# A chunked attention recurrence and its MLP: four small matrix products laid into quarters of TensorE, denser loads of a, r and v, and a new order of all engines

## The chip, the cores and the metric

The kernel runs on one core of a Trainium2 chip. The metric is the device time of one execution in microseconds (us), as a median of several runs. The engines are named as in the profile: PE (TensorE, matrix products; PEld is its loading of weights), DVE (VectorE), ACT (ScalarE), POOL (GpSimd) and SP (SyncE, which here only issues transfers).

## What is computed

For each of 4 x 8 heads a 40 x 40 state goes through 768 steps; the outputs of all heads, 320 numbers a token, then go through an MLP:

```python
for t in range(S):
    y[:, :, t] = np.einsum('bhd,bhde->bhe', rt, state)
    Sa = np.einsum('bhde,bhe->bhd', state, at)
    state_decay = state * wt[:, :, None, :] - np.einsum('bhd,bhe->bhde', Sa, bt)
    state = state_decay + np.einsum('bhd,bhe->bhde', vt, kt)
...
x = np.ascontiguousarray(attn_out.transpose(0, 2, 1, 3)).reshape(B * S, H * D)
a = x @ w1
b = x @ w2
h = a * b @ w3
return (h @ w_out).astype(np.float32)
```

S = 768, D = 40, B = 4, H = 8; w1 and w2 are 320 x 1024, w3 1024 x 1024, w_out 1024 x 320. The MLP's weights arrive as 64-bit floats.

## The kernel before, in words

The 768 steps are cut into 12 chunks c of 64 tokens. The 32 heads are 16 pairs: a batch entry is a group g (four of them) of four pairs p, and a pair's two heads lie in partitions 0 to 39 and 64 to 103 (`ab` = 0, 1 in the code). Of each chunk these steps are made, the first ones for each group:

- `load` (L369) fetches w, b and k (`fm`) and a (`lh`, which stands twice, each time with one head's rows filled and the other's zero).
- `scale` (L374): a running product of w on DVE (L386), its logarithm and inverse on ACT (L390, L393), and with these a (L397) and b, k (L408, "x scaling") are multiplied; L397 and L408 are on DVE or POOL by a letter per chunk in `ON`.
- `causal` (L420): one full-array product per pair of scaled b, k with scaled a (L431). ACT copies parts of it into `JP` and the rest back into `lh`, where POOL cuts off the upper triangle (L449).
- `solve` (L455), once for the chunk's 16 pairs together: the inverses of the triangular 64 x 64 matrices, by some 40 DVE instructions that wait for one another, from the transpose L463 (which reads all four groups' `JP`) to the transposes L538 and L541 (which write `TDX`). `join` (L545) completes the inverses with two PE products (L564, L571) and ACT copies into `TT`.
- `pairs` (L591): r times v, the "small products" (L608), copied by ACT and cut by POOL (L616). `tokens` (L620) transposes b and k on PE (L631).
- `rec` (L636), the recurrence itself: state (L647, the state `SB` times r and a's identity part), two ACT copies into `xu`; f2 (L654), a copy into `hs`; inverse (L661, `TT` times `hs`); two masks on DVE back into `xu` (L665); f5 (L672); the new state and y on DVE (L689, L706), a transpose on PE (L695), two copies into `SB`.
- `gather` (L710) collects y by transfers into `xr`, and `mlp` (L727), some two chunks later, has 16 products with W1, W2 (L758, eight matmuls each), DVE products of the two (L772), `gh` and the rest `gl` (L775), and eight products with W3 w_out (L784).

At the start `weights` (L310) turns the 64-bit weights into pairs of floats: 33 pieces of 128 x 512 go through `convert` (L268), four or five passes on DVE, two on ACT and one on POOL (L298). The product of w3 and w_out is made once (L351). The MLP of the first chunk waits for all of them.

PE lays the shapes out as follows: L431, L647, L631, L695 and the MLP use the full array; L654 and L672 two column halves; L608 and L661 two of the four 64 x 64 quarters beside each other; L564 and L571 two of the 32 x 32 parts.

The order of all instructions is not written out by hand. Every operation is given an engine, a cost and a due time (`Order.op`, L70); `place` (L89) puts them one by one, always the one that can start first and among these the one due first, with the buffers of `SLOTS` (L30) and the costs as its clock. What comes out is fixed as a queue for each engine, in that order. `T` and `P` (L35, L36) hold the due times.

Of the kernel before, what the change touches and what calls it, by code (L numbers as in the profile page):

```python
# [24 lines left out]
TOK = B * C  # L25
W65 = C + 1
WMAX, GMIN = 1.5, 2.0 ** -40
CW = 512
LAT = dict(pe=0.33, act=0.09, dve=0.09, pool=0.1, sp=3.0, nil=0.0)
SLOTS = dict(fm=8, lh=6, gi=2, gt=1, ab=1, TDX=1, rv=3, xu=3, bk=3, hs=2, st=2, y=1, xr=1, JP=2, TT=2, bank=6,  # L30
# [4 lines left out]
T0, T = 29.92, 49.86  # L35
P = dict(w0=14.16, ws=3.0, ld=73.16, sc=53.09, ca=46.04, so=7.66, sp=36.36, jo=7.42, pa=12.28, tk=5.03, rg=13.65,  # L36
         ga=35.51, ml=86.47, mt=47.69)

ON = dict(cv="p", ws="d", lh="ppddpppppddp", xs="pppdpppppppd", gl="pppdpddddddd")


class Slot:


    def __init__(self, order, pool):
        self.order, self.pool, self.at, self.left, self.since, self.until = order, pool, None, 0, 0.0, 0.0
        if order.direct:
            self.at = order.turn[pool] = (order.turn.get(pool, -1) + 1) % SLOTS[pool]

    @property  # L50
    def t(self):
        return self.order.tiles[self.pool][self.at]


class Order:
# [11 lines left out]
    def slot(self, pool):  # L67
        return Slot(self, pool)

    def op(self, eng, cost, due, fn, r=(), w=(), two=False, kind=None, hold=()):  # L70
# [11 lines left out]
        slots = {k[0] if isinstance(k, tuple) and isinstance(k[0], Slot) else k for k in (*r, *w, *hold)}  # L82
        slots = [s for s in slots if isinstance(s, Slot)]
        for s in slots:
            s.left += 1
        self.ops.append(dict(n=n, eng=eng, cost=cost, due=due, fn=fn, deps=deps - {None, n}, slots=slots, two=two,
                             kind=kind))

    def place(self):  # L89
# [28 lines left out]
        placed = []  # L118
        while len(placed) < len(ops):
            best = None  # L120
            for e in LAT:
                starts = [(t, o) for o in ready[e] if (t := begin(o)) is not None]
                if starts:
                    first = min(t for t, _ in starts)
                    o = min((o for t, o in starts if t <= first + 1e-9), key=lambda o: (o["due"], o["n"]))
                    if best is None or first < best[0]:
                        best = first, o
            if best is None:
                raise ValueError(f"stuck after {len(placed)} of {len(ops)}: " + str([(e, o["due"], o["fn"].__qualname__, [(s.pool, s.at) for s in o["slots"]]) for e in LAT for o in sorted(ready[e], key=lambda o: o["due"])[:4]]) + str({p: len(f) for p, f in free.items()}))
            t, o = best  # L130
            e = o["eng"]
            ready[e].remove(o)
            cost = o["cost"]
            if e == "pe":
                cost += 0.1 * (o["kind"] != last)
                last = o["kind"]
            for s in o["slots"]:
                if s.at is None:
                    at = min(free[s.pool])
                    free[s.pool].remove(at)  # L140
                    s.since, s.at = at
# [3 lines left out]
            done = clock[e] + LAT[e]  # L145
            o["start"], o["end"] = t, clock[e]
            placed.append(o)
            for s in o["slots"]:
                s.until, s.left = max(s.until, done), s.left - 1
                if not s.left:  # L150
                    free[s.pool].append((s.until, s.at))
            for u in o["users"]:
                u["wait"] -= 1
                u["ready"] = max(u["ready"], clock[e] if u["eng"] == e != "sp" else done)
                if not u["wait"]:
                    ready[u["eng"]].append(u)
        self.placed = sorted(placed, key=lambda o: (o["start"], o["n"]))
# [4 lines left out]
def attention_moe(ctx: ExitStack, tc: tile.TileContext, fmx, fma, rv, vt, sq, svr, w12, w3t, wo, out):  # L162
# [44 lines left out]
    SB = cp.tile([104, NPC, 104], F32, name="SB")  # L207
# [9 lines left out]
    for name, shape in dict(fm=[104, 772], lh=[128, 2, NP, C], gi=[104, NP, C], gt=[104, NP, C],   # L217
                            TDX=[128, 1024], rv=[104, NP, 2 * C + D], xu=[128, 2, NP, C + D], bk=[128, NP, 104],
# [48 lines left out]

    def convert(src, dst, due, w=()):  # L268

        n = src.shape[1]  # L270
        raw, e, sg, mf = slot("raw"), slot("e"), slot("sg"), slot("mf")

# [21 lines left out]
        def f7():  # L294
            dve.tensor_tensor(out=sg.t[:, 0:n], in0=sg.t[:, 0:n], in1=e.t[:, 0:n].bitcast(BF16), op=ALU.mult)
# [4 lines left out]
        op("sp", 0.6, due - 8, f1, w=[raw])  # L300
# [4 lines left out]
        op("dve", 0.64, due, f6, r=[raw], w=[mf], two=True)  # L305
        op("dve", 0.38, due, f7, r=[e], w=[sg], two=True)
        both(ON["cv"], 1.25, 0.62, due, f8, r=[sg, "conv"], w=[mf] if dst is None else [mf, *w])
        return mf

    def weights():  # L310

        due, step = P["w0"], P["ws"]
        for k in range(3):
# [13 lines left out]
            for f in range(2048 // CW):  # L327
                cs = slice(CW * f, CW * f + CW)
                mf = convert(w12[k * 128:k * 128 + 128, cs], None, due)
                n = (0, 1, 4)[k]  # L330
                rows = slice(64, 128) if k == 2 else slice(0, 128)
                over = ["conv"] if k == 0 else ["conv", "reg2"]

                def f1(mf=mf, n=n, cs=cs):
                    copy(WT[n][:, cs], mf.t)

                def f2(e, mf=mf, n=n, rows=rows, k=k, cs=cs):
                    e.tensor_tensor(out=WT[2 + k][rows, cs], in0=mf.t[rows], in1=WT[n][rows, cs], op=ALU.subtract)
# [22 lines left out]
    fm_, lh_, jp_, tt_, xu_, rv_, bk_, y_, xr_, tdx_ = ({} for _ in range(10))  # L361
# [7 lines left out]
    def load(c, g, due):  # L369
        fm, lh = fm_[c, g], lh_[c, g] = slot("fm"), slot("lh")  # L370
        op("sp", 0.6, due, lambda: sp.dma_start(out=fm.t, in_=fmx[c, g]), w=[(fm, "g"), (fm, "x")])
        op("sp", 0.4, due, lambda: sp.dma_start(out=lh.t[0:104], in_=fma[c, g]), w=[(lh, 0), (lh, 1)])

    def scale(c, g, due):  # L374

        fm, lh, gi, gt = fm_[c, g], lh_[c, g], slot("gi"), slot("gt")
# [18 lines left out]
        def f5(e):  # L395
            a = lh.t[0:104]
            e.tensor_tensor(out=a, in0=a, in1=gam(c, g)[:, :, 0:C].unsqueeze(1).to_broadcast([104, 2, NP, C]), op=ALU.mult)  # L397
# [17 lines left out]
        both(ON["lh"][c], 1.2, 0.62, due + 1, f5, r=[G], w=[(lh, 0), (lh, 1)])  # L415
        op("dve", 0.42, due + 2, f6, r=[G, gi], w=[gt], two=True)
        op("dve", 0.45, due + 2, f7, r=[gt], w=[gi], two=True)
        both(ON["xs"][c], 1.35, 0.62, due + 3, f8, r=[gi], w=[(fm, "x")])

    def causal(c, g, due):  # L420

        fm, lh, jp, pt = fm_[c, g], lh_[c, g], jp_[c], slot("bank")
        ns = slice(g * NP, g * NP + NP)

        def bank():
            return pt.t.rearrange("p (n x t) -> p n x t", n=NP, x=2)

        def f1():
            X = x12(c, g)
            for p in range(NP):  # L430
                pe.matmul(out=bank()[:, p], lhsT=X[:, p].rearrange("q x t -> q (x t)"), rhs=lh.t[0:104, :, p],  # L431
                          start=True, stop=True)

        op("pe", 0.92, due, f1, r=[(fm, "x"), (lh, 0), (lh, 1)], w=[pt], kind="128", hold=[jp])
        for ab in range(2):
            q = 64 * ab
            op("act", 0.39, due + 1, lambda q=q, ab=ab: copy(
                jp.t[q:q + 32, ns], bank()[q:q + 32, :, ab].rearrange("q p (x t) -> q p x t", x=2)),
               r=[pt], w=[(jp, g, 2 * ab)])
            op("act", 0.29, due + 1, lambda q=q, ab=ab: copy(  # L440
                jp.t[q + 32:q + 64, ns, 0], bank()[q + 32:q + 64, :, ab, 32:64]), r=[pt], w=[(jp, g, 2 * ab + 1)])
        for ab in range(2):
            q = slice(64 - 64 * ab, 128 - 64 * ab)

            def f2(q=q, ab=ab):
                copy(lh.t[q, ab], bank()[q, :, ab], -1.0)
# [5 lines left out]
            op("act", 0.4, due + 4, f2, r=[pt], w=[(lh, ab)])  # L452
            op("pool", 0.5, due + 6, f3, w=[(lh, ab)], two=True)

    def solve(c, due, span):  # L455
# [28 lines left out]
        def dots(out_, x, y, shape, slow=1.0):  # L484
# [30 lines left out]
        for z in range(2):  # L515
# [3 lines left out]
                 lambda r0=r0: A()[:, r0:r0 + 8, r0 + 8:r0 + 16].unsqueeze(2), (8, 4, 8), 1.8)  # L519
# [439 lines left out]
```

## Time and profile before

| | |
|---|---|
| median of 3 runs | 761.85 us (759.58, 761.85, 767.97) |
| the profiled execution | 762.65 us, of which the span of the profile is 760.9 |
| busy: PE, weight loads, DVE, ACT, POOL | 650.0, 584.3, 597.3, 474.0, 249.7 us |
| chain of work that ended last | PE 61%, DVE 25%, transfers 8%, ACT 3% |
| transferred | 70.29 MB in 57,937 packets, mean 92 GB/s |
| per issue: fm, rv, lh, a piece of weights | 313.6, 273.0, 208.0, 512.0 KB |

A row of groups reads: line, engine, operation, output <- inputs, shapes, count | busy us, mean ns of one | idle time just before them and what ended it. A row of the timeline: start, duration, then the same. PE's instructions overlap, so how long one holds the engine is read from start to start. A float product is two passes, so two MATMUL records: L661 has 16 for its eight products.

### The profile page before, as it was taken

The numbers are of one execution on the slowest core, as the hardware profiler recorded it, in microseconds if no ns is written. First come the engines' busy times: TensorE is split into PE (matmuls) and PEld (weight loads), VectorE is DVE, ScalarE is ACT, GpSimd is POOL, SyncE is SP. The second block draws the span as 40 slices with busy tenths as digits, with TensorE's granted clock in tenths as the row PEclk, the third lists the DMA queues.
The fourth block names the chain that finished last, engine by engine and source line by source line (L and its number), as shares of the span: only waits on it lengthen the run. The fifth ranks groups of instructions, "written<-read, shape, count | busy, mean of one in ns | idle before, by whom it ended". The sixth has DMA issues, their size and how long they took to land.

```text
span 760.9 us, 20122 instructions
## 1 busy us (share of the span) xinstructions
PE 650.0 (85%) x7954; PEld 584.3 (77%) x7954; DVE 597.3 (78%) x1173; ACT 474.0 (62%) x1127; POOL 249.7 (33%) x330
## 2 busy tenths in 40 slices
PE   2323777848689999999999998999999999999996
PEld 1312655636579889898899987998989989998996
DVE  5679989999989985895978967968898799783321
ACT  3474575456767568676696775775957768654331
POOL 3356333544424154362433622513223222100000
PEclk9955669968779999999999999999999999999999
DMA  8922364623440151532424324224243242210010
GB/s 205 262 70 67 118 182 152 178 85 108 110 114 15 32 148 38 134 86 71 109 68 119 81 55 108 83 69 122 58 109 90 68 111 80 48 52 19 21 28 20
DMA packets 57937, 70.29 MB, mean 92 GB/s; under 512 B 30960, under 2 KB 38640, under 8 KB 57840
## 3 DMA queue, kind: packets, MB, share of 16 engines
q1 hardware_dynamic: 57840, 68.97, 33.6%
q8 instruction: 64, 1.05, 0.6%
q14 instruction: 33, 0.27, 0.1%
HBM read 60.29 MB, written 3.93 MB: 84 GB/s over the span
## 4 chain that ended last, share of the span: by engine, by line
PE 61%; DVE 25%; DMA 8%; ACT 3%; issue 2%; SPq 0%; DVEq 0%
PE bank L758 21%; PE bank L784 10%; PE bank L431 5%; PE bank L654 4%; PE bank L647 4%; PE bank L661 4%; PE bank L672 4%; DVE tmp L489 3%; DVE mf L291 3%; PE bank L608 3%; DMA fm<-in_fmx_dram 2%; DMA rv<-in_rv_dram 2%; DVE xu L665 2%; DMA lh<-in_fma_dram 2%; PE bank L695 2%
## 5 line engine op out<-in xcount | busy, mean ns | idle before, releaser
L758 PE MATMUL bank<-xs,W 128*128 128x256 f32 x1536 | 214.5, 289 | 1.0 <-ACT lh L173 1.0
L758 PEld LDWEIGHTS bank<-xs,W 128*128 128x128 f32 x1536 | 191.0, 190 | 7.2 <-issue 2.4
L173 ACT ACTIVATE xu<-bank 64x256 f32<-64x256 f32 (+2 forms) x184 | 80.3, 441 | 47.2 <-PE bank L647 21.1
L616 POOL TENSOR_SCALAR_AFFINE_SELECT xu<-xu 64x256 f32<-64x256 f32 x96 | 45.1, 470 | 143.2 <-ACT xu L173 122.3
L173 ACT ACTIVATE JP<-bank 32x256 f32<-32x256 f32 (+1 forms) x216 | 75.7, 351 | 22.4 <-PE bank L431 17.6
L408 POOL TENSOR_TENSOR fm<-fm,gi 104x512 f32<-104x512 f32 x40 | 57.7, 1441 | 69.4 <-DVE gi L404 60.7
L431 PE MATMUL bank<-lh,fm 104*128 104x128 f32 x384 | 59.6, 305 | 22.1 <-POOL fm L408 16.0
L665 DVE TENSOR_TENSOR xu<-bank,mask_h 64x416 f32<-64x416 f32 x96 | 56.2, 585 | 25.9 <-PE bank L661 24.1
L431 PEld LDWEIGHTS bank<-lh,fm 104*128 104x128 f32 x384 | 53.3, 214 | 24.7 <-POOL fm L408 16.8
L449 POOL TENSOR_SCALAR_AFFINE_SELECT lh<-lh 64x256 f32<-64x256 f32 x96 | 42.8, 445 | 85.0 <-ACT lh L173 70.9
L784 PE MATMUL bank<-W3h,gh 128*128 128x320 f32 x192 | 63.0, 328 | 0.0
L608 PE MATMUL bank<-rv 40*64 40x64 f32 x768 | 34.9, 234 | 29.4 <-DMA rv<-in_rv_dram 27.7
L784 PE MATMUL bank<-W3l,gh 128*128 128x320 f32 x192 | 59.3, 309 | 0.0
L784 PE MATMUL bank<-W3h,gl 128*128 128x320 f32 x192 | 59.2, 308 | 0.0
L654 PE MATMUL bank<-xu,lh 128*64 128x104 f32 (+2 forms) x768 | 49.8, 274 | 10.8 <-POOL xu L616 5.5
L397 POOL TENSOR_TENSOR lh<-lh,fm 104x512 f32<-104x512 f32 x32 | 39.5, 1234 | 53.4 <-DMA lh<-in_fma_dram 27.9
L772 DVE TENSOR_TENSOR ga<-bank,ga 128x512 f32<-128x512 f32 x48 | 32.8, 684 | 30.4 <-PE bank L758 24.9
L608 PEld LDWEIGHTS bank<-rv 40*64 40x64 f32 x768 | 28.1, 143 | 36.8 <-DMA rv<-in_rv_dram 28.2
L654 PEld LDWEIGHTS bank<-xu,lh 128*64 128x64 f32 (+2 forms) x768 | 39.9, 147 | 17.8 <-issue 7.1
L672 PE MATMUL bank<-xu,bk 128*40 128x104 f32 (+1 forms) x768 | 47.7, 259 | 6.6 <-DVE xu L665 6.5
L661 PE MATMUL bank<-hs,TT 64*64 64x104 f32 x768 | 46.4, 265 | 3.1 <-ACT hs L173 1.8
L173 ACT ACTIVATE gh<-ga 128x512 fp32r<-128x512 f32 x48 | 30.1, 628 | 29.5 <-DVE ga L772 29.2
(96 smaller groups left out, 1408.8 us busy)
## 6 DMA issues: line engine op xcount, KB each, us to landing
fm<-in_fmx_dram SPq DMA_DIRECT2D x48, 313.6 KB
rv<-in_rv_dram SPq DMA_DIRECT2D x48, 273.0 KB
lh<-in_fma_dram SPq DMA_DIRECT2D x48, 208.0 KB
raw<-in_w3t_dram SPq DMA_DIRECT2D x16, 512.0 KB
raw<-in_w_dram SPq DMA_DIRECT2D x12, 512.0 KB
xu<-in_vt_dram SPq DMA_DIRECT2D x96, 40.0 KB
out_dram<-o SPq DMA_DIRECT2D x48, 80.0 KB
xr<-y SPq DMA_DIRECT2D x72, 40.0 KB
```

The lines of the kernel that those rows point to most:

```text
L173: act.activation(out_, in_, AF.Copy, scale=scale)
L408: e.tensor_tensor(out=X, in0=X, in1=gi.t.unsqueeze(2).to_broadcast([104, NP, 2, C]), op=ALU.mult)
L431: pe.matmul(out=bank()[:, p], lhsT=X[:, p].rearrange("q x t -> q (x t)"), rhs=lh.t[0:104, :, p], start=True, stop=True)
L449: pool.affine_select(out=lh.t[q, ab], in_=lh.t[q, ab], pattern=[[0, NP], [1, C]], compare_op=ALU.is_gt, fill=0.0, base=0, channel_multipli ...
L608: pe.matmul(out=bank()[64 - 64 * ab:128 - 64 * ab, p, 0:C], lhsT=rvt.t[r, p, C + D:], rhs=rvt.t[r, p, 0:C], start=True, stop=True)
L616: op("pool", 0.5, due + 2, lambda q=q, ab=ab: pool.affine_select(out=xu.t[q, ab, :, 0:C], in_=xu.t[q, ab, :, 0:C], pattern=[[0, NP], [1, C ...
L654: pe.matmul(out=view(hp)[64 * ab:64 * ab + 64, p], lhsT=lh.t[k, ab, p], rhs=xu.t[k, ab, p], start=True, stop=True)
L661: pe.matmul(out=view(hh)[r, p], lhsT=tt.t[r, n0 + p], rhs=hs.t[r, p], start=True, stop=True)
L665: dve.tensor_tensor(out=xu.t[r, ab], in0=view(hh)[r], in1=mask_h[r].unsqueeze(1).to_broadcast([64, NP, N]), op=ALU.mult)
L672: pe.matmul(out=view(qs)[r, p], lhsT=bk.t[:, p, r], rhs=xu.t[:, ab, p], start=(c == 0), stop=True, skip_group_check=True)
L758: pe.matmul(out=pt.t[:, TOK * x:TOK * x + TOK], lhsT=WT[k][:, cs], rhs=xs.t[:, z], start=(n == 0), stop=(n == 7))
L784: pe.matmul(out=pt.t[:, 0:DM], lhsT=l.t[:, j, ts], rhs=W3[r][:, j], start=(j == 0 and n == 0), stop=(j == NJ - 1 and n == 2))
```

## The change

What the code does now:

- causal, state and inverse are made of 64 x 64 quarters, like the small products; the four quarters are issued in the order of `QUADS`, and the two row halves write to two PSUM banks beside each other. Causal is 16 smaller products instead of four. The state `SB` is stored as halves (104 x 8 x 2 x 64 instead of 104 x 16 x 104).
- a recurrence holds a slot of two banks (`bank2`) from its state to its y; the inverse writes into the same two banks. No more than two recurrences are under way (`rc`). The masks of L665 are four over half the elements (L767).
- a is loaded dense into `al` (two transfers of 40 partitions) and multiplied into `lh` (L483); r and v dense into `rv` (two transfers), whose identity part is written once. The lower rows of W1, W2 are loaded and converted once and copied (`split`), so 31 pieces are converted instead of 33.
- the planner has new costs and rules (a changed kind of PE work, a reserve of banks, the transfers' own time), and `T`, `P` and `ON` have new values. a's scaling is on POOL in all chunks, `gl` on POOL in the first ten, some passes of the conversion change engine.

In the diff's core:

```diff
+QUADS = (0, 0), (1, 1), (0, 1), (1, 0)
...
-T0, T = 29.92, 49.86
-P = dict(w0=14.16, ws=3.0, ld=73.16, sc=53.09, ca=46.04, so=7.66, sp=36.36, jo=7.42, pa=12.28, tk=5.03, rg=13.65,
-         ga=35.51, ml=86.47, mt=47.69)
-
-ON = dict(cv="p", ws="d", lh="ppddpppppddp", xs="pppdpppppppd", gl="pppdpddddddd")
+T0, T = 45.21, 43.48
+P = dict(w0=12.33, ws=4.09, ld=74.23, sc=40.83, ca=45.61, so=5.62, sp=45.27, jo=3.71, pa=8.34, tk=5.31, rg=14.14,
+         ga=3.91, ml=91.39, kp=1.58, mt=25.16, mg=10.0)
+
+ON = dict(cv="pppppppppppdddppppdpppppdpdpppp", ws="d", lh="pppppppppppp", xs="dpppppdppppp", gl="ppppppppppdd",
+          cb="dddddddddddddddddddpdpddddddppp")
...
             X = x12(c, g)
             for p in range(NP):
-                pe.matmul(out=bank()[:, p], lhsT=X[:, p].rearrange("q x t -> q (x t)"), rhs=lh.t[0:104, :, p],
-                          start=True, stop=True)
+                for ab, x in QUADS:
+                    r = slice(64 * ab, 64 * ab + 40)
+                    pe.matmul(out=bank(ab)[64 * x:64 * x + 64, p], lhsT=X[r, p, x], rhs=lh.t[r, ab, p], start=True,
+                              stop=True)
...
         def f1():
-            for p in range(NP):
-                pe.matmul(out=view(qs)[0:104, p], lhsT=SB[:, n0 + p], rhs=rvt.t[:, p, 0:N], start=(p == 0), stop=False,
-                          skip_group_check=True)
+            for u in range(2):
+                for h, ab in QUADS:
+                    r, m = slice(64 * h, 64 * h + 40), 64 - 24 * ab
+                    pe.matmul(out=q(slice(64 * ab, 64 * ab + m), 2 * h + u), lhsT=SB[r, n0 // 2 + u, ab, 0:m],
+                              rhs=rvt.t[r, u, ab, C:2 * C + D], start=(u == 0), stop=False, skip_group_check=True)
...
         def f3():
-            for p in range(NP):
-                for ab in range(2):
-                    r = slice(64 * ab, 64 * ab + 64)
-                    pe.matmul(out=view(hh)[r, p], lhsT=tt.t[r, n0 + p], rhs=hs.t[r, p], start=True, stop=True)
-
-        def f4(ab):
-            r = slice(64 * ab, 64 * ab + 64)
-            dve.tensor_tensor(out=xu.t[r, ab], in0=view(hh)[r], in1=mask_h[r].unsqueeze(1).to_broadcast([64, NP, N]),
-                              op=ALU.mult)
+
+            for p in range(0, NP, 2):
+                for ab, x in QUADS:
+                    r, k = slice(64 * ab, 64 * ab + 64), p + (ab ^ x)
+                    at = 512 * ab + 256 + N * (p // 2)
+                    pe.matmul(out=qs.t[64 * x:64 * x + 64, at:at + N], lhsT=tt.t[r, n0 + k], rhs=hs.t[r, k],
+                              start=(c == 0), stop=True, skip_group_check=True)
+
+        def f4(ab, x):
+            r, k = slice(64 * x, 64 * x + 64), ab ^ x
+            dve.tensor_tensor(out=xu.t[64 * ab:64 * ab + 64, ab, k:NP:2],
+                              in0=qs.t[r, 512 * ab + 256:512 * ab + 256 + 2 * N].rearrange("p (n t) -> p n t", n=2),
+                              in1=mask_h[r].unsqueeze(1).to_broadcast([64, 2, N]), op=ALU.mult)
...
-            a = lh.t[0:104]
-            e.tensor_tensor(out=a, in0=a, in1=gam(c, g)[:, :, 0:C].unsqueeze(1).to_broadcast([104, 2, NP, C]), op=ALU.mult)
+
+            full = [104, 2, NP, C]
+            e.tensor_tensor(out=lh.t[0:104], in0=al.t.unsqueeze(1).to_broadcast(full),
+                            in1=gam(c, g)[:, :, 0:C].unsqueeze(1).to_broadcast(full), op=ALU.mult)
```

Line numbers in the new code: causal L520, join L653 and L660, small products L697, state L746, f2 L753, inverse L762, masks L767, f5 L775, new state and y L798 and L816; solve from L552 to L630; MLP L869 and L895. The numbers behind names (bank_152) tell buffers apart; a `bank_` of the new order is a pair of banks.

How the order moves, on PE behind the join of a middle chunk. Before, from the first join product to the first MLP product behind the second (JP and TDX are the solved chunk's, fm_103 belongs to the next one's last group):

```order
L564 MATMUL bank_141<-TDX_113,JP_129 32x32 x32
L431 MATMUL bank_138<-lh_107,fm_103 128x128 x4
L647 MATMUL bank_142<-rv_115,SB 104x104 x4
L571 MATMUL bank_141<-TDX_113,JP_129 32x32 x32
L784 MATMUL bank_143<-W3h,gh_1609 128x320
```

The last causal product of the next chunk (L431) stands right behind the first join product. Now, at the same place of a middle chunk, behind the two join products, three MLP products and two states (fm_98 and fm_99 are the next chunk's last two groups):

```order
L753 MATMUL bank_152<-xu_121,lh_108 64x104 x8
L753 MATMUL bank_152<-xu_122,lh_109 64x104 x8
L762 MATMUL bank_154<-hs_127,TT_136 64x104 x8
L520 MATMUL bank_152<-lh_108,fm_98 64x64 x16
L762 MATMUL bank_153<-hs_128,TT_136 64x104 x8
L775 MATMUL bank_154<-xu_121,bk_124 40x104 x8
L722 MATMUL bank_152<-ident,fm_103 128x104 x4
L775 MATMUL bank_153<-xu_122,bk_125 40x104 x8
L520 MATMUL bank_152<-lh_109,fm_99 64x64
```

The next chunk's last two causal products have moved behind the recurrences of two groups; each is made from the `lh` buffer (108, 109) that the f2 (L753) in the same list reads before.

On DVE, from the second transpose of a solve to the first instruction of the next. Before:

```order
L541 STREAM_TRANSPOSE TDX_113<-TDX_113 128x512
L744 TENSOR_TENSOR xs_1611<-xr_128,xs_1611 128x768
L397 TENSOR_TENSOR lh_105<-lh_105,fm_99 104x512
L463 STREAM_TRANSPOSE ab<-JP_129 128x1024
L489 TENSOR_TENSOR tmp<-DG,ab 128x4
```

Now:

```order
L630 STREAM_TRANSPOSE TDX_117<-TDX_117 128x512
L471 SCALAR_TENSOR_TENSOR fm_99<-fm_99,first 104x260
L855 TENSOR_TENSOR xs_1806<-xr_132,xs_1806 128x768
L487 TENSOR_TENSOR gt_116<-fm_99,gi_115 104x256
L491 SCALAR_TENSOR_TENSOR gi_115<-gt_116,gi_115 104x256
L767 TENSOR_TENSOR xu_121<-bank_154,mask_h 64x2x104 x4
L767 TENSOR_TENSOR xu_122<-bank_153,mask_h 64x2x104 x4
L798 TENSOR_TENSOR st_129<-bank_154,fm_100 104x160
L816 TENSOR_TENSOR y_131<-bank_154,fm_100 104x4x64
L798 TENSOR_TENSOR st_130<-bank_153,fm_101 104x160
L816 TENSOR_TENSOR y_131<-bank_153,fm_101 104x4x64
L552 STREAM_TRANSPOSE ab<-JP_133 128x1024
```

The masks, states and outputs of two groups' recurrences now stand between two solves; the MLP's split and a scaling stood there before.

More of the change, by code (lines that the diff above doesn't have):

```diff
@@ L51, in t, with pick @@
     def t(self):
-        return self.order.tiles[self.pool][self.at]
+        return self.order.tiles["bank2"][self.at // 2] if self.two else self.order.tiles[self.pool][self.at]
+    def pick(self, free, t):
+        if self.two:
+            pairs = [(max(free[i], free[i + 1]), i) for i in free if i % 2 == 0 and i + 1 in free]
+            if not pairs:
+                return None
+            since, i = min(pairs)
+            return since, [i, i + 1]
+        if not free:
+            return None
+        i = min(free, key=lambda i: (max(free[i], t), self.pool == "bank" and i ^ 1 in free, free[i], i))
+        return free[i], [i]
 class Order:
@@ L95, in place @@
                 ops[d]["users"].append(o)
-        free = {p: [(0.0, i) for i in range(n)] for p, n in SLOTS.items()}
+        free = {p: dict.fromkeys(range(n), 0.0) for p, n in SLOTS.items()}
         ready = {e: [] for e in LAT}
-        clock, last, lock = dict.fromkeys(LAT, 0.0), None, {"dve": 0.0, "pool": 0.0}
+        clock, last, lock, dma = {**dict.fromkeys(LAT, 0.0), "pool": 8.0, "dve": 4.0, "sp": 1.0}, None, {"dve": 0.0, "pool": 0.0}, 0.0
         for o in ops:
@@ L116, in begin, with choice @@
             return t
-        placed = []
+        uses = {p: {o["eng"] for o in ops for s in o["slots"] if s.pool == p} for p in SLOTS}
+        placed, cand, spare = [], {}, {}
+        def choice(e, starts):
+            if not starts:
+                return None
+            first = min(t for t, _ in starts)
+            return first, min((o for t, o in starts if t <= first + 1e-9),
+                              key=lambda o: (o["due"] - P["kp"] * (e == "pe" and o["kind"] == last), o["n"]))
         while len(placed) < len(ops):
@@ L132, in place @@
             ready[e].remove(o)
+            stale = {e, *(("dve", "pool") if o["two"] else ())}
             cost = o["cost"]
             if e == "pe":
-                cost += 0.1 * (o["kind"] != last)
+                cost += 0.1 * (o["kind"] != last and "mlp" in (o["kind"], last)) + 0.04 * (o["kind"] != last)
                 last = o["kind"]
@@ L150, in place @@
                 if not s.left:
-                    free[s.pool].append((s.until, s.at))
+                    stale |= uses[s.pool]
+                    for i in range(s.at, s.at + 1 + s.two):
+                        free[s.pool][i] = s.until
             for u in o["users"]:
@@ L224, in attention_moe @@
         dve.memset(t, 0.0)
+    for t in tiles["al"]:
+        dve.memset(t[32:64], 0.0)
+    for t in tiles["rv"]:
+        for h in range(2):
+            q = slice(64 * h, 64 * h + 40)
+            pool.tensor_copy(out=t[q].rearrange("q u x n -> q (u x) n")[:, :, 2 * C:],
+                             in_=ident[q, q].unsqueeze(1).to_broadcast([40, 4, D]))
     tmp = ap_.tile([128, 1024], F32, name="tmp")
@@ L264, in both @@
                    r=r, w=w, two=True)
+    count = [0]
     def convert(src, dst, due, w=()):
@@ L271, in convert @@
         raw, e, sg, mf = slot("raw"), slot("e"), slot("sg"), slot("mf")
+        k = count[0]
+        count[0] += 1
         def f1():
@@ L445, in f2 @@
             def f2(q=q, ab=ab):
-                copy(lh.t[q, ab], bank()[q, :, ab], -1.0)
+                copy(lh.t[q, ab], bank(ab)[q], -1.0)
             def f3(q=q, ab=ab):
```

273 lines of the change are left out of this document (165 added, 108 removed).

## The prediction

> **What bounds the kernel now.** I read the share of busy time in six stages first, then PE's and DVE's timelines in one steady chunk, then DVE's waits. The stages (busy us of PE, weight loads, DVE, ACT, POOL; clock; DMA share; GB/s):
>
> ```profile
> 0.00:38.00 38.00, 10.34 (x84) 9.60 (x84) 23.02 (x45) 14.29 (x32) 13.09 (x24) 1.00 0.89 234
> 38.00:220.70 182.70, 115.13 (x1083) 88.91 (x1081) 166.93 (x309) 109.34 (x248) 80.75 (x90) 0.73 0.40 118
> 220.70:294.10 73.40, 69.55 (x846) 64.72 (x846) 67.87 (x131) 51.75 (x129) 30.03 (x36) 1.00 0.28 72
> 294.10:646.30 352.20, 347.39 (x4626) 319.70 (x4626) 288.19 (x595) 251.63 (x623) 119.64 (x167) 1.00 0.34 88
> 646.30:753.90 107.60, 107.50 (x1329) 101.32 (x1328) 51.13 (x95) 46.65 (x97) 6.16 (x13) 1.00 0.13 31
> ```
>
> Up to 220.7, where the last weight is converted, DVE sets the pace (91% busy after the transfers of the first 38 us). The seven chunks from the join at 294.1 to that at 646.3 take 50.3 us each, with PE 99% busy. The tail is PE alone. So PE looks like the whole answer from 294 on. But a second loop is as long:
>
> ```profile
> 595.87 0.71 DVE L541 STREAM_TRANSPOSE TDX<-TDX 128x512 f32<-128x512 f32 x1
> ...
> 601.48 2.04 DVE L463 STREAM_TRANSPOSE ab<-JP 128x1024 f32<-128x1024 f32 x1 [3.46 <-ACT JP L173]
> ...
> 644.56 0.71 DVE L541 STREAM_TRANSPOSE TDX<-TDX 128x512 f32<-128x512 f32 x1
> ```
>
> On DVE a chunk's solve runs from L463 to L541 (601.5 to 645.3, 43.8 us, other chunks' work in between), PE joins it, and the next chunk's L463 follows 4.9 us after the last L541, as soon as ACT has copied that chunk's JP. 43.8 + 4.9 = 48.7: DVE's queue is in order, so this loop stands 1 to 2 us behind PE's. Relief on PE is worth no more than that, unless the loop shrinks too. The nine solve parts that end in the fourth to the twelfth join (sum of their durations, and of DVE's busy time in them):
>
> ```profile
> sum 371.49, DVE 339.32; mean DVE 37.70
> ```
>
> **PE's part of the change.** From start to start on PE's timeline:
>
> ```profile
> 420.12 0.93 PE L661 MATMUL bank<-hs,TT 64*64 64x104 f32 x16
> 420.98 1.22 PE L758 MATMUL bank<-xs,W 128*128 128x256 f32 x8
> 422.03 0.89 PE L647 MATMUL bank<-rv,SB 104*104 104x104 f32 x8
> 422.86 0.92 PE L672 MATMUL bank<-xu,bk 128*40 128x104 f32 x16
> ...
> 424.84 0.68 PE L608 MATMUL bank<-rv 40*64 40x64 f32 x16
> 425.45 0.54 PE L695 MATMUL bank<-ident,st 104*40 104x104 f32 x4
> ...
> 427.84 1.05 PE L431 MATMUL bank<-lh,fm 104*128 104x128 f32 x8
> 428.65 2.14 PE L758 MATMUL bank<-xs,W 128*128 128x256 f32 x16
> ...
> 435.65 0.90 PE L647 MATMUL bank<-rv,SB 104*104 104x104 f32 x8
> 436.32 1.21 PE L758 MATMUL bank<-xs,W 128*128 128x256 f32 x8
> ```
>
> State takes 0.67 before an operation of the same array shape and 0.83 before another shape: a change of shape costs 0.16. Inverse is 0.86 - 0.16 = 0.70 for sixteen passes of 104 columns, two beside each other, 87 ns a round; small products 0.61 - 0.16 = 0.45, causal 0.81. With four beside each other, inverse and state are four rounds, 0.35 (two at a time: 0.70). Causal is 32 passes: eight rounds of 57 ns are 0.45, the pace of L564 below (64 passes in 1.13, 17.7 ns) gives 0.57; I take 0.53, and 0.27 for small products. A group saves 0.28 + 0.32 + 0.35 + 0.18 = 1.13, a chunk 4.5. Against it the order has 235 changes of shape in seven chunks, not 201 (+0.8 a chunk), and 21 steps from an MLP product to another full-array operation, not 63, of 0.08 each (-0.5; 420.98 to 422.03 is 1.05 where the two in a row from 428.65 need 0.95 each). PE falls from 347.39/7 = 49.6 to 45.4 us a chunk. If PE alone counted, eight chunks would save some 35 us.
>
> **The loop's part.** In the new order two groups' whole recurrences stand between the join and the last two causal products of the next chunk; before, one causal product stood right behind the join. From the end of the second transpose (L541, now L630), by PE's prices, that last causal starts at 11.4 at the earliest. Waits come on top. What ACT does there:
>
> ```profile
> L173 ACT ACTIVATE xu<-bank 64x416 f32<-64x416 f32 x44 | 22.3, 507 | 26.5 <-PE bank L647 21.1 <-PE bank L672 4.9
> ...
> L173 ACT ACTIVATE TT<-bank 32x512 f32<-32x512 f32 x24 | 14.0, 585 | 3.8 <-PE bank L571 3.6
> L173 ACT ACTIVATE o<-bank 128x320 f32<-128x320 f32 x24 | 10.5, 436 | 23.2 <-PE bank L784 22.9
> ```
>
> The second join ends at 4.3. ACT then has two TT copies (1.17), an output copy (0.44) and four copies of the two states (2.05): 8.0, where PE could have been at 6.8. The first group's f2 runs from 7.0, its copy into hs (as long as one into xu) ends at 8.5, its inverse starts behind the second f2, at 8.9, and ends at 9.45. DVE, idle since 3, now masks:
>
> ```profile
> L665 DVE TENSOR_TENSOR xu<-bank,mask_h 64x416 f32<-64x416 f32 x96 | 56.2, 585 | 25.9 <-PE bank L661 24.1
> ...
> L706 DVE TENSOR_TENSOR y<-bank,fm 104x256 f32<-104x256 f32 x48 | 19.9, 416 | 3.7 <-PE bank L672 3.6
> ...
> L408 DVE TENSOR_TENSOR fm<-fm,gi 104x512 f32<-104x512 f32 x8 | 7.7, 965 | 0.2
> ```
>
> A mask over half the elements costs between 0.29 (half of 585 ns) and 0.416 (256 elements at L706); 0.38 by elements. Eight are 3.1: f5 of the second group starts at 12.5, the last causal at 13.3. From a causal's start to the next L463 it was 2.74 (598.74 to 601.48); the new causal is 0.3 shorter, and I take 2.1: the gap is 15.4 instead of 4.9.
>
> ```profile
> 598.74 1.09 PE bank L431 x8
> ...
> 684.19 1.13 PE bank L564 x64
> ```
>
> In return the solve part holds less: 68 DVE instructions (39 of the solve, 13 of the gates, 8 half masks, 4 MLP products, 4 for state and y; no gl, no a-scaling). Priced at the means of their forms they are 35.5 us; the same count over the nine parts of before gives 370.7 against the 371.5 measured, so the price includes usual waits. 1.5 of these were waits for L661 (10.6 us in the seven chunks), which now stands well ahead: 34.0. The bounds are 32.7 (no waits, by 339.32/371.49) and 35.5. **The loop is 15.4 + 34.0 = 49.4 us a chunk**, against 49.2 on average in the eight of before (253.0 to 646.3), and PE, 45.4 with 1.9 of waits in the gap, stands idle for 2. DVE's total hardly changes (-0.79 a-scaling, -1.73 gl, +1.40 masks a chunk).
>
> **The start.** Counted likewise, DVE has 225.4 instead of 233.5 us ahead of the third join (two conversions less, some multiplications on POOL, against quarter masks): 7.6 us at that stretch's busy share. Dense a, r, v shorten what stands ahead of the weights:
>
> ```profile
> DVE fm L381 <- DMA fm<-in_fmx_dram: 7.2, 3, 4.1
> DVE e L277 <- DMA raw<-in_wo_dram: 5.6, 2, 3.4
> ```
>
> Of these 12.8 us I take 5 (bounds 0 and 12.8): some 1.2 MB less at 234 GB/s. The third join was at
>
> ```profile
> 253.00 1.20 PE L564 MATMUL bank<-TDX,JP 32*32 32x32 f32 x64 [0.82 <-DVE TDX L541]
> ```
>
> and comes at 253.0 - 12.6 = 240.4.
>
> **The sum.** 240.4 + 8 x 49.4 = 635.6 for the eleventh join; + 3.0 for the one chunk whose four x scalings are on DVE (L408 above, less what overlaps); the last loop is shorter, 15.4 + 25.0; the tail from the twelfth join was 753.9 - 684.2 = 69.7, less 2.4 of PE prices, plus 1.9 of waits in its gap; 7.0 behind PE's end. 755.2, and 1.75 around the span (762.65 for 760.9): **757 us**. The profiled execution lay 0.8 above the median of 761.85.
>
> **Rivals.** (1) PE decides after all: waits in the gap are covered and the solve part runs at 32.7, so the loop is 47.0, what PE needs with its waits. 8 x 2.4 = 19 less: 738. For it: PE was 99% busy; against it: the causal products' place in the queue. (2) The start gains all 12.8 and a little on DVE: 749. (3) Narrow passes have a floor of 25 ns: causal 0.80, state and inverse 0.40, so 0.74 in the gap, 763; against it the 17.7 ns of L564. The Trainium skill, "TensorE: Matmul & The Clock Gate", section "Wait — 56ns, not 53.3ns?", has start to start never below some 25 ns; L564's row here disagrees. (4) **Slower**: the gap's causal products need lh, which POOL can write only once f2 has released it:
>
> ```profile
> L397 POOL TENSOR_TENSOR lh<-lh,fm 104x512 f32<-104x512 f32 x32 | 39.5, 1234 | 53.4 <-DMA lh<-in_fma_dram 27.9 <-DVE xu L665 11.8 <-DVE fm L381 4.2
> ```
>
> 1.23 us behind the f2 of 7.9 just meets PE at 9.3. Each us that POOL is late, as it would be behind one gl or x product, is a us of the loop; at 1.9 late it is 51.3, 772, and from 1.6 on the kernel is slower by over 1%. That quarters run only two at a time, so that the change does not do what it says, ends alike: +2.0 in the gap, 773. L661 (different rows and columns) and L654 (same rows, different columns) each show two side by side, none shows four.
>
> **Chances.** Forecast 0.47, rival 1 0.27, rival 2 0.07, rival 3 0.06, rival 4 0.13 (POOL 0.08, quarters 0.05). A measurement of this kernel tells about 1% from no change. The forecast's own spread (gap and solve part each by 1 us, so 745 to 768) puts a quarter of it below 754.2: faster 0.45, same 0.39, slower 0.16. The range reaches from a little below rival 1 to rival 4: 733 to 773.
>
> **What would show it.** In the profile of after: operations of state and inverse 0.35 apart without a change of shape, 0.5 with one; PE below 93% busy between the fourth and eleventh joins, waiting at L653 for DVE; 15 us from L630 to L552 with DVE idle for some 6 before L767; a period of 49.4. A PE that is 98% busy there, or an L552 within 12 us of L630, makes the forecast wrong.

## The result: 863.5 us, 13% slower, and the profile after

The changed kernel takes 863.49 us (median, 858.18 to 864.86) against 762.44 for the kernel before: a ratio of 1.130, interval 1.122 to 1.138. Forecast were 757 us and a range of 733 to 773. The profiled execution took 863.63, its span is 861.8.

The stages of the kernel after, cut at the starts of the joins (busy us of PE, weight loads, DVE, ACT, POOL; clock; DMA share; GB/s):

```profile
241.90:302.60 60.70, 52.29 (x784) 44.63 (x784) 38.70 (x87) 36.43 (x94) 22.42 (x29) 0.89 0.22 57
302.60:358.70 56.10, 47.29 (x787) 40.39 (x786) 39.32 (x89) 36.95 (x97) 22.38 (x28) 1.00 0.24 61
358.70:427.50 68.80, 58.78 (x804) 50.97 (x804) 41.45 (x92) 37.21 (x98) 18.04 (x25) 0.83 0.20 50
...
599.70:655.70 56.00, 47.19 (x785) 40.34 (x784) 39.24 (x89) 36.83 (x97) 22.39 (x28) 1.00 0.24 61
655.70:716.10 60.40, 52.02 (x785) 44.60 (x785) 39.30 (x89) 37.04 (x97) 22.36 (x28) 0.89 0.22 54
716.10:768.50 52.40, 43.88 (x679) 37.39 (x680) 31.65 (x71) 27.65 (x69) 11.58 (x16) 0.93 0.14 34
768.50:855.80 87.30, 72.33 (x821) 64.18 (x820) 21.73 (x42) 25.45 (x53) 2.93 (x5) 1.00 0.07 18
```

No engine is full: PE is busy for 84% of a chunk of 56 us (99% before), DVE for 70%. Four of the eight chunks take 56.0 to 56.1 us, at a clock of 1.00; the others, with the same work but for the four x scalings on DVE in the one of 68.8, take 60 to 69 at 0.83 to 0.89. The last stage, 69.7 us of PE work alone before, is 87.3 now, and PE is idle for 15 of it.

By the terms of the sum (the third column is the first experiment, below; us):

| term | forecast | after | six tiles |
|---|---|---|---|
| third join | 240.4 | 241.9 | 230.4 |
| gap from the end of L630 to L552, steady chunk | 15.4 | 18.1 | 15.6 to 16.2 |
| solve part, L552 to the end of L630 | 34.0 | 38.0, 41 to 50 where the clock is low | 34.0 to 34.7 |
| third to eleventh join, eight chunks | 398.2 | 474.2 | 406.2 |
| eleventh to twelfth join | 40.4 | 52.4 | 43.0 |
| twelfth join to the end of the span | 76.2 | 93.3 | 74.5 |

The 106.6 us between forecast and profiled execution are thus 1.5 at the start, 76.0 in the eight chunks, 12.0 in the last loop and 17.1 behind it. Of the 76.0, 53 are a loop of 56.1 instead of 49.4; 23 lie in the chunks with a low clock.

DVE's timeline in an undisturbed gap of the kernel after:

```profile
598.03 0.69 DVE L630 STREAM_TRANSPOSE TDX<-TDX 128x512 f32<-128x512 f32 x1
...
603.20 0.42 DVE L491 SCALAR_TENSOR_TENSOR gi<-gt,gi 104x256 f32<-104x256 f32 x1
610.08 3.09 DVE L767 TENSOR_TENSOR xu<-bank,mask_h 64x208 f32<-64x208 f32 x8 [6.45 <-PE bank L762]
...
616.80 1.99 DVE L552 STREAM_TRANSPOSE ab<-JP 128x1024 f32<-128x1024 f32 x1 [1.91 <-ACT JP L225]
```

The picture is the forecast one (two recurrences in the gap, DVE idle for some 6 us ahead of the masks), only longer. Why it is longer shows in the two engines that follow the first group's f2 there:

```profile
606.21 2.53 PE L753 MATMUL bank<-xu,lh 128*64 128x104 f32 x32 [0.30 <-ACT xu L225]
...
607.76 2.32 POOL L483 TENSOR_TENSOR lh<-al,fm 104x512 f32<-104x512 f32 x2 [2.77 <-PE bank L753]
...
608.78 0.93 ACT L225 ACTIVATE hs<-bank 128x416 f32<-128x416 f32 x2 [1.02 <-PE bank L753]
609.35 0.39 PEld L762 LDWEIGHTS bank<-hs,TT 64*64 64x64 f32 x16 [0.81 <-ACT hs L225]
```

The 32 passes are the f2 of two groups. POOL overwrites the first group's `lh` at 607.76, so that f2 is done. ACT is free at 607.77 (four xu copies from 605.65, 2.12), yet the copy of that same f2 into hs starts 1.02 later, when the second group's f2 is done too. The waits of the whole kernel, summed (waiting instruction, releaser: us, times, longest), hold more of these:

```profile
ACT SB L225 <- PE bank L869: 22.5, 23, 1.4
ACT hs L225 <- PE bank L697: 6.7, 9, 0.9
PE bank L869 <- ACT ga L225: 5.9, 8, 0.7
PE bank L869 <- ACT SB L225: 5.4, 14, 0.4
```

A copy into `SB` reads the transpose L805, and hs the f2; neither reads an MLP product or a small product. An MLP product reads neither SB nor ga. In the kernel before, the same copies waited for their own producer:

```profile
ACT SB L173 <- PE bank L695: 23.7, 24, 2.7
```

And in the stage of MLP products alone, PE of the kernel after stops after every second product:

```profile
807.43 2.16 PE L869 MATMUL bank<-xs,W 128*128 128x256 f32 x16 [0.75 <-ACT ga L225]
810.45 2.15 PE L869 MATMUL bank<-xs,W 128*128 128x256 f32 x16 [0.85 <-DVE ga L883]
```

What such pairs share is a tile. Six banks of PSUM were six tiles of 128 x 512; to let a recurrence span two banks, the new code declares three tiles of 128 x 1024 and hands out halves, and the order shown ahead of the prediction knows `bank_152`, `bank_153` and `bank_154` alone. In the built program the wait of that first hs copy names a count of PE's semaphore (5044) that only the second group's f2, in the other half, completes; the first group's ends at 5036.

**Theory T1**: the program waits by tile, so that an instruction on one bank waits for products and copies of its neighbour; the planner counts six free banks and writes an order that these waits break. Rivals: **T2**, the loop through DVE's queue is simply longer than priced; **T3**, the new rule for the choice of a bank (`pick` prefers the half whose neighbour is busy) takes a bank again too soon.

### The profile page after: what moved, and what is told of

The parts are those of the page before. It is cut to its first block, busy times and chain, and to the rows that moved or that the text cites. A ratio compares the mean times of both kernels' runs of the same rounds, so it can differ in the third digit from the quotient of the medians.

```text
span 861.8 us, 23475 instructions
## 1 busy us (share of the span) xinstructions
PE 658.4 (76%) x9458; PEld 553.4 (64%) x9458; DVE 579.5 (67%) x1226; ACT 485.3 (56%) x1221; POOL 290.5 (34%) x373
## 4 chain that ended last, share of the span: by engine, by line
PE 52%; DVE 26%; ACT 14%; issue 3%; DMA 3%; SPq 0%; DVEq 0%; ACTq 0%
PE bank L869 20%; PE bank L895 8%; DVE tmp L578 5%; PE bank L426 4%; PE bank L753 4%; PE bank L775 3%; DVE ga L883 3%; ACT JP L225 3%; ACT xu L225 3%; PE bank L697 2%; DVE xu L767 2%; PE bank L805 2%; ACT SB L225 2%; DVE Tp L582 2%; PE bank L520 2%
## 5 line engine op out<-in xcount | busy, mean ns | idle before, releaser
L869 PE MATMUL bank<-xs,W 128*128 128x256 f32 x1536 | 229.0, 303 | 22.6 <-ACT ga L225 5.9
L869 PEld LDWEIGHTS bank<-xs,W 128*128 128x128 f32 x1536 | 204.3, 203 | 37.1 <-ACT SB L225 8.3
L767 DVE TENSOR_TENSOR xu<-bank,mask_h 64x208 f32<-64x208 f32 x192 | 71.3, 371 | 117.6 <-PE bank L762 107.1
L225 ACT ACTIVATE xu<-bank 64x128 f32<-64x128 f32 (+2 forms) x280 | 88.9, 343 | 38.6 <-PE bank L869 15.3
L483 POOL TENSOR_TENSOR lh<-al,fm 104x512 f32<-104x512 f32 x48 | 57.5, 1207 | 72.2 <-PE bank L753 62.3
L886 POOL TENSOR_TENSOR gl<-ga,gh 128x512 fp32r<-128x512 f32 x40 | 52.9, 1322 | 76.5 <-ACT gh L225 51.2
L753 PE MATMUL bank<-xu,lh 104*64 104x104 f32 (+2 forms) x768 | 60.1, 296 | 21.1 <-ACT xu L225 10.8
L895 PE MATMUL bank<-W3h,gh 128*128 128x320 f32 x192 | 62.9, 328 | 9.8 <-DVE ga L883 8.8
L753 PEld LDWEIGHTS bank<-xu,lh 104*64 104x64 f32 (+2 forms) x768 | 46.9, 161 | 33.1 <-ACT xu L225 21.5
L895 PE MATMUL bank<-W3h,gl 128*128 128x320 f32 x192 | 59.3, 309 | 0.0
L895 PE MATMUL bank<-W3l,gh 128*128 128x320 f32 x192 | 59.3, 309 | 0.0
L520 PE MATMUL bank<-lh,fm 40*64 40x64 f32 x1536 | 38.3, 241 | 25.8 <-POOL fm L495 9.6
L775 PE MATMUL bank<-xu,bk 128*40 128x104 f32 (+1 forms) x768 | 47.4, 269 | 12.9 <-DVE xu L767 12.9
L722 PE MATMUL bank<-ident,fm 104*128 104x104 f32 x192 | 29.3, 279 | 34.3 <-DMA al<-in_fma_dram 11.5
L426 PE MATMUL bank<-wof,w3f 128*128 128x320 f32 x128 | 45.8, 510 | 11.9 <-ACT bk L225 6.3
L520 PEld LDWEIGHTS bank<-lh,fm 40*64 40x64 f32 x1536 | 31.7, 150 | 33.1 <-issue 12.7
```

The lines of the kernel that those rows point to most:

```text
L225: act.activation(out_, in_, AF.Copy, scale=scale)
L426: pe.matmul(out=pt.t[:, 0:DM], lhsT=w[:, j], rhs=wof[:, j], start=(j == 0), stop=(j == NJ - 1))
L483: e.tensor_tensor(out=lh.t[0:104], in0=al.t.unsqueeze(1).to_broadcast(full), in1=gam(c, g)[:, :, 0:C].unsqueeze(1).to_broadcast(full), op= ...
L520: pe.matmul(out=bank(ab)[64 * x:64 * x + 64, p], lhsT=X[r, p, x], rhs=lh.t[r, ab, p], start=True, stop=True)
L753: pe.matmul(out=view(hp)[64 * ab:64 * ab + 64, p], lhsT=lh.t[k, ab, p], rhs=xu.t[k, ab, p], start=True, stop=True)
L767: dve.tensor_tensor(out=xu.t[64 * ab:64 * ab + 64, ab, k:NP:2], in0=qs.t[r, 512 * ab + 256:512 * ab + 256 + 2 * N].rearrange("p (n t) -> p ...
```

## Experiments

**1. Six tiles again.** The order of operations is the same; what spans two banks is issued once for each:

```diff
-    tiles["bank2"] = [ps.tile([128, 1024], F32, name=f"bank{i}") for i in range(SLOTS["bank"] // 2)]
-    tiles["bank"] = [t[:, 512 * i:512 * i + 512] for t in tiles["bank2"] for i in range(2)]
+    tiles["bank"] = [ps.tile([128, 512], F32, name=f"bank{i}") for i in range(SLOTS["bank"])]
...
-copy(halves(xu.t[r, ab]), wide(qs, N)[r])
+[copy(xu.t[r, ab, 2 * h:2 * h + 2], wide(qs, N)[h][r]) for h in range(2)]
```

> The new kernel in the same order of operations, but the six PSUM banks are six tiles again instead of halves of three tiles. A recurrence still holds two neighbouring banks; the instructions that read both (two copies into xu, the new state, y) become two each over half the elements, so this version has more work: four short ACT copies for two longer ones and four DVE instructions for two, some 1.4 us of ACT and 1.4 us of DVE a chunk. Theory T1 (instructions wait for the other half of a two-bank tile, which they neither read nor write: copies wait for a neighbour's products, products for a neighbour's copies): the steady loop falls from 56.1 to 52 to 54 us a chunk, the PE clock stays at 1.00 from 260 us on, so no chunk takes 60, and the part behind the twelfth join falls from 86 to about 74: some 790 us (775 to 810). Theory T2 (the causal products behind two recurrences on an in-order DVE are all of it, and the tiles do not matter): the loop grows by the added work to 57 to 58, 865 to 885. Theory T3 (a bank is taken again too soon, by the rule that picks the half whose neighbour is busy): the picks are the same, so no faster than 860.

Measured: 755.03 us (753.7 to 755.89), a ratio to before of 0.992 (0.989 to 0.994). 108 us of the kernel after are gone, more than T1 had forecast (775 to 810), although this version has more instructions. T2 and T3 do not survive as causes of the slowdown. The same place of a gap:

```profile
542.85 0.99 PE L753 MATMUL bank<-xu,lh 104*64 104x104 f32 x16 [0.18 <-ACT xu L226]
543.86 2.36 POOL L483 TENSOR_TENSOR lh<-al,fm 104x512 f32<-104x512 f32 x2 [1.99 <-PE bank L753]
...
544.22 0.52 ACT L226 ACTIVATE hs<-bank 128x416 f32<-128x416 f32 x1
544.88 0.39 PEld L762 LDWEIGHTS bank<-hs,TT 64*64 64x64 f32 x16
544.98 0.52 ACT L226 ACTIVATE hs<-bank 128x416 f32<-128x416 f32 x1 [0.24 <-PE bank L753]
```

The first hs copy follows its own f2 (ACT was with xu copies until 544.20) and no longer the second, whose copy has its own wait at 544.98. The waits across banks are gone from the list, SB waits 2.8 us for its transpose, and MLP products run without a stop:

```profile
ACT SB L226 <- PE bank L805: 2.8, 10, 0.6
```

```profile
710.78 7.89 PE L869 MATMUL bank<-xs,W 128*128 128x256 f32 x64
```

The eight chunks and the stage behind the twelfth join:

```profile
230.40:636.60 406.20, 376.00 (x6273) 327.19 (x6272) 319.12 (x770) 290.67 (x829) 175.44 (x220) 0.99 0.26 67
...
679.60:747.90 68.30, 67.52 (x820) 63.30 (x820) 21.68 (x45) 27.76 (x64) 2.93 (x5) 1.00 0.10 25
```

**2. Paired tiles in the kernel before.** The reverse, and nothing else:

```diff
-    tiles["bank"] = [ps.tile([128, 512], F32, name=f"bank{i}") for i in range(SLOTS["bank"])]
+    pairs = [ps.tile([128, 1024], F32, name=f"bank{i}") for i in range(SLOTS["bank"] // 2)]
+    tiles["bank"] = [t[:, 512 * i:512 * i + 512] for t in pairs for i in range(2)]
```

> The kernel before, with nothing changed but the declaration of PSUM: six banks as halves of three two-bank tiles, as in the new kernel. T1: slower by far, 790 to 840 us, PE waiting in L758 for ACT copies of other operations, and its granted clock below 1.00 at times. T2 and T3: the same as before within 1%, 762.

Measured: 842.16 us against 761.51 before, 1.107 (1.103 to 1.111): 81 us for one declaration. Products wait for copies of other operations, as in this piece of PE's timeline behind the third join:

```profile
266.02 1.21 PE L759 MATMUL bank<-xs,W 128*128 128x256 f32 x8 [0.68 <-ACT JP L173]
...
273.46 2.08 PE L759 MATMUL bank<-xs,W 128*128 128x256 f32 x8 [1.27 <-ACT TT L173]
```

L759 here is before's L758. The second of the two, eight passes, takes 2.08 us instead of 1.21: the clock has fallen as well. So the cost comes with the declaration, in both kernels and in both directions.

**3 and 4. The rule for the choice of a bank.** `pick` as before, the bank that has been free longest, once with the paired tiles and once with six:

```diff
-key=lambda i: (max(free[i], t), self.pool == "bank" and i ^ 1 in free, free[i], i)
+key=lambda i: (free[i], i)
```

> The new kernel with the rule of before for the choice of a bank (the one that has been free longest); the order of operations is the same, only bank numbers differ. T1: neighbouring banks still share a tile, so most waits stay: 840 to 862, with the 0.75 us waits in the MLP products of the end (behind every second product) at half their number. T2: 863 within 1%. T3: these waits vanish, the part behind the twelfth join falls from 86 to 74, and the whole to 830 to 845.

> Six tiles and the old rule together. T1: as the six tiles alone within 8 us. T3: at least 15 us less than the six tiles alone. T2: 865 to 885.

Measured: 869.74 us with paired tiles (868.54 to 871.25), 0.7% slower than the kernel after. That is above what T1 and T3 had said; it lies in T2's "863 within 1%", but T2 had fallen with experiment 1. From the twelfth join to PE's end it takes 76.2 us instead of 87.3, so there the rule matters, as T1 and T3 both had it; but five of its chunks take 60.7 to 62.2 us (half clock for 13.7 or 17.1 us in each). With six tiles it is 754.81 (754.7 to 755.81), as with the new rule: T3 is out.

**5 and 6. Is the loop through DVE what bounds the six tiles?** The causal products of two groups are made three times, once of the two groups whose product stands in the gap, once of the other two:

```diff
-            for p in range(NP):
+            for p in list(range(NP)) * (3 if g >= 2 else 1):
...
+            for p in list(range(NP)) * (3 if g < 2 else 1):
```

> Six tiles, and the causal products of each chunk's third and fourth group made three times over (the same values written again), which adds two times 0.45 to 0.49 us of PE to each of the two that stand between a join and the next solve, 1.8 to 2.0 us a chunk. Theory T2 (with six tiles the loop over DVE's queue, gap plus solve part, sets the time, and the last causal product ends the gap): gap and loop grow by 1.4 to 2.0 us, nine loops of them make 13 to 18: 768 to 773 us. Theory T4 (PE's amount of work sets the time): 12 x 1.9 = 22 more: 777. Theory T5 (DVE's amount of work sets it): 755 within 1%.

> The same two threefold causal products a chunk, but of the first and second group, which stand in the middle of the solve part: the same number of added PE passes, 1.8 to 2.0 us a chunk, at a place where only PE has them. T2: hidden, loop longer by 0 to 0.5 us: 755 to 760. T4: 777, as in the run before. T5: 755.

Measured: 777.00 us (774.11 to 779.94; the profiled execution's span is 772.4) in the gap, 765.97 (762.0 to 768.15) elsewhere. Both lie above what T2 had said (768 to 773 and 755 to 760), and the first is T4's 777; but T4 had 777 for the second as well. The stretch from the third to the eleventh join, first in the one kernel, then in the other:

```profile
232.00:653.60 421.60, 389.13 (x7299) 341.04 (x7298) 320.54 (x770) 291.19 (x830) 175.39 (x220) 0.99 0.26 65
```

```profile
231.80:646.90 415.10, 389.78 (x7299) 342.03 (x7299) 322.80 (x769) 289.39 (x828) 172.80 (x220) 0.99 0.26 66
```

The same PE work costs 15.4 us over the eight chunks in the gap (1.9 each; the steady gap grows from 15.7 to 17.7) and 8.9 elsewhere (1.1 each; the gap stays, the solve part grows from 34.2 to 35 to 36). T4 and T5, for which the place does not matter, are out; T2 holds for the gap. Elsewhere the time was not hidden, but only a part of it is waiting for PE. Over the eight chunks DVE's waits for PE grow by 2.8 us, those for transfers of w, b, k by 2.6, and its own busy time by 3.7 (322.80 for 319.12) with the same instructions. The last comes from L491, first with six tiles alone, then here:

```profile
L491 DVE SCALAR_TENSOR_TENSOR gi<-gt,gi 104x256 f32<-104x256 f32 x31 | 19.8, 638 | 3.0
```

```profile
L491 DVE SCALAR_TENSOR_TENSOR gi<-gt,gi 104x256 f32<-104x256 f32 x31 | 26.1, 841 | 2.9
```

One L491 takes 0.42 us, but 1.2 to 1.3 when a product on POOL (L483 or L886) runs beside it; that is so for 8 of the 31 with six tiles alone and for 15 here, as in this piece:

```profile
482.77 1.42 POOL L886 TENSOR_TENSOR gl<-ga,gh 128x512 fp32r<-128x512 f32 x1 [1.44 <-issue]
483.15 1.32 DVE L491 SCALAR_TENSOR_TENSOR gi<-gt,gi 104x256 f32<-104x256 f32 x1
```

So a part of the cost is that the passes added on PE shifted DVE's instructions against POOL's.

**7, 8 and 9. Other orders with six tiles.** All three let a state be made ahead of its chunk's join, give the split copies their true costs, and have other due times; 7 and 9 have eight buffers `lh`:

```diff
-SLOTS = dict(rc=2, fm=8, al=4, lh=6,
+SLOTS = dict(rc=2, fm=8, al=4, lh=8,
...
-r=[("SB", g), (rvt, 0), (rvt, 1), bk, *ins], w=[qs]
+r=[("SB", g), (rvt, 0), (rvt, 1), bk, *parts[2:]], w=[qs]
```

> Six tiles and another order: eight buffers lh instead of six, a state may be made before its chunk's join, costs of the split copies as they are, and due times and engine letters that were chosen so that the last causal products stand earlier. In this order fewer of the recurrences' instructions stand between two solves and more inside the solve part. T2: the gap falls from 15.7 to 10 to 12 us, the solve part grows from 34 to 37 to 39, the loop falls from 50.2 to 46 to 49: 715 to 745 us. T4: PE has the same amount of work, 755 within 1%. T5: the loop falls only as far as DVE's busy time allows, which is 39.7 us a chunk, so the same as T2 here.

Measured: 762.78 us, ratio 1.000 (0.998 to 1.003), a miss. The gap fell to 10 to 13 us as expected, but the solve part grew to 38.5 to 42 and the loop is 51.4, no shorter than the 50.8 of six tiles alone. DVE is busy in it for 43.4 us a chunk (347.34 in eight; 39.9 with six tiles alone):

```profile
234.90:645.90 411.00, 370.11 (x6271) 328.67 (x6269) 347.34 (x804) 293.61 (x833) 133.30 (x188) 0.97 0.26 66
```

The engine letters had been chosen with the order, and had moved work from POOL to DVE, the gl subtractions above all:

```profile
L884 DVE TENSOR_TENSOR gl<-ga,gh 128x512 fp32r<-128x512 f32 x28 | 19.0, 678 | 2.0 <-ACT gh L224 2.0
```

In the eight chunks it is 28 more than with six tiles alone, in the whole kernel 24 more (32 of 48 for 8 of 48; the 36 in the expectation of run 9 below is a miscount). Four scalings of a add 2.8 us, and a step of the solve (L599) takes 1.28 us for 0.39, eight times. The clock is also lower, 0.97 for 0.99. The next two runs put the letters back.

> Six tiles, six buffers lh and the engine letters of the new kernel, so DVE has the same instructions as in the run with six tiles alone; a state may be made ahead of its chunk's join, the split copies have their true costs in the order, and the due times are others, chosen for a short loop. T2: the gap keeps its two recurrences and stays at 15 to 16 us, but PE waits less inside the solve part, which falls to 33: loop 48 to 49.5 instead of 50.2, 735 to 750 us. T6 (DVE's busy time of 40 us a chunk and the waits of an in-order queue take back what any such order gives, as in the run before): 755 to 765.

Measured: 758.74 us, 0.996 (0.993 to 0.998): in T6's range, not in T2's. DVE has no more work than with six tiles alone (318.06 us in the eight chunks), but its waits have changed places. In the whole kernel it waits 24.6 us for the inverse instead of 64.9, but it waits longer for ACT's part of the MLP's split (L850; 6.2 us with six tiles alone) and for transfers of w, b and k (4.3 us there):

```profile
DVE xs L853 <- ACT xs L850: 36.5, 8, 5.6
DVE fm L464 <- DMA fm<-in_fmx_dram: 21.8, 22, 2.5
```

Its clock in the eight chunks is 0.96. Which of these keeps the loop at 51.7 us is not shown; the waits for transfers alone do not, for run 9 has as many (22.9 us) and is faster.

> As the run with the causal products earlier (eight buffers lh, state ahead of the join), but with the rest gl back on POOL as in the new kernel: in that run 36 of 48 gl had stood on DVE, 28 more than here, of 0.69 us each, 1.7 us a chunk. T2: the gap is 8 to 14 us (one of 19), the solve part 37 to 39, the loop 47 to 49: 725 to 745 us. T6: 755 to 765. If it is as slow as that run (763), the gl on DVE were not what took the gain back.

Measured: **741.22 us** (739.12 to 743.49), 0.972 (0.965 to 0.979): faster than the kernel before by 2.8% and than the kernel after by 14%. The eight chunks take 48.3 us each; the mean gap is 11 us, the mean solve part 37, and PE is busy for 96% of the time:

```profile
241.60:628.00 386.40, 369.29 (x6235) 325.69 (x6229) 314.98 (x774) 289.33 (x823) 165.57 (x217) 1.00 0.28 70
```

So this order is worth 2.5 us a chunk against six tiles alone (406.2 less 386.4, in eight). Its causal products stand earlier, but its states, its buffers `lh` and its due times differ too, so what the place of the causal products is worth by itself is not shown. Runs 7 and 9 differ in due times and in the clock (0.97 and 1.00) as well as letters, so that the letters alone made the difference is likely, not shown.

## Why the prediction was wrong, point by point

- **The step that failed** is the waits in "The loop's part" and in the tail: I let every operation wait for its data, its buffer and its engine, and took the "usual waits" of before for the rest. That two banks of one tile wait for each other stood nowhere in the sum, though the change declares it and the new order names three bank buffers where there had been six. Experiments 1 and 2 price this at 108 and 81 us. None of the rivals was this one; the slower rivals ended at 773. Of the signs of "What would show it" only the period and the gap failed (56.0 us at its shortest for 49.4, 18.1 for 15.4); PE below 93% busy, DVE idle for 6 us ahead of L767 and no L552 within 12 us of L630 all appeared in a kernel 106 us slower than forecast, so they could not point at this cause.
- **The clock adds to it.** The sum has prices at a clock of 1.00 and no term for a fall. In the kernel after, chunks of the same instructions take 56.0 to 56.1 us without and 60.1 to 60.8 with a time at half clock, 23 us in all with the chunk of 68.8. With six tiles the eight chunks run at 0.99. The share was read from chunks of one trace, not tested by itself.
- **The loop through DVE** was right where the tiles do not interfere: gap 15.6 to 16.2 for 15.4, solve part 34.0 to 34.7 for 34.0, PE 92.6% busy (below 93% was forecast), and experiment 5 says that what is added to the gap lengthens the loop by as much. The 755.0 us of six tiles beside the 757 forecast are partly luck: the third join came 10.0 us earlier than forecast, the eight chunks took 8.0 longer, the last loop 2.6 longer.
- **The start.** 253.0 became 230.4 with six tiles, 22.6 us earlier; I took 12.6 and had 20.4 as the upper bound, so rival 2's start came, and more. Paired tiles take 11.5 of it back. The parts of the gain were not separated.
- **PE's prices** were right where operations stand side by side, with six tiles: two states in a row span 0.94 us, the last pass's 0.25 included, so 0.35 each for 16 passes; L762 is followed by another shape after 0.52 (forecast 0.5), the quartered causal after 0.63 (forecast 0.69). Half a mask takes 371 ns (0.38). The sum of PE's work was not right: PE is busy for 47.0 us a chunk (376.00 in eight) where 45.4 was forecast. Part of the 1.6 is the end of the last pass ahead of each wait, which counts as busy; the rest was not separated.
- **The rivals.** PE alone (738) is refuted by the loop of 50 us with PE 92.6% busy. A floor of 25 ns and quarters that run only in pairs are refuted by the 0.35: 22 ns a pass. By the Trainium skill, "TensorE: Matmul & The Clock Gate", section "Wait — 56ns, not 53.3ns?", starts would not come closer than about 25 ns. In these quarters they do. POOL is not late with lh: with six tiles both scalings (543.86 to 546.22) are done 3 us ahead of the last causal product at 549.42.

## What to carry to other kernels

When a change lays buffers together, read what the program waits by: if it is the tile, two halves used by different work are one buffer for every wait, whatever a planner counts. The sign in a trace is a wait whose releaser shares no data with the waiting instruction, and the proof is one declaration, undone in the new kernel and done in the old. And where the time is set by a loop through an in-order queue, work moved out of its gap is only gained if it does not come back inside the loop.

## What the runs showed of the hardware

PE's clock fell to half without any long pause. PE's timeline of the kernel after ahead of the first such time in its chunks, at 260.6, and in it:

```profile
258.22 0.59 PE L746 MATMUL bank<-rv,SB 40*64 40x104 f32 x16
259.94 0.58 PE L722 MATMUL bank<-ident,fm 104*128 104x104 f32 x4 [1.14 <-ACT SB L225]
260.35 1.84 PE L869 MATMUL bank<-xs,W 128*128 128x256 f32 x8
...
269.63 2.07 PE L869 MATMUL bank<-xs,W 128*128 128x256 f32 x8
```

The longest pause in the 6.8 us ahead is this 1.14 us; eight MLP passes then take 2.07 us instead of 1.21, and the half clock lasts 13.7 us. The clock of this trace changes only at steps of 3.41 us (its times at half clock are 3.41, 6.83, 10.24, 13.65 or 17.07 us long). In the last such step ahead of the fall PE was busy for 66%, but another step with 59% had no such effect (kernel after; length, PE's busy time and passes, clock, DMA share, GB/s):

```profile
257.23:260.65 3.42, 2.27 (x34) 1.00 0.72 155
496.17:499.58 3.41, 2.01 (x74) 1.00 0.45 115
```

The Trainium skill, "TensorE: Matmul & The Clock Gate", section "Why this matters for your kernels", asks for no idle time of PE above about 3 us between bursts of matmuls if the clock is not to drop. Here it dropped after pauses of at most 1.14 us. What sets the limit was not settled.

DVE's L491, 0.42 us by itself, took 1.2 to 1.3 us beside a product on POOL (experiment 6), while the masks L767 took 0.37 us with and without one.
